# A transformer's attention layer: where weights are measured, and which score blocks go to VectorE

## The chip, the cores and the metric

The kernel runs on one core of a Trainium2 chip. The core has TensorE (matrix products, PE in the profile; its weight loads are PEld), VectorE (DVE), ScalarE (ACT), GpSimd (POOL) and SyncE (SP, which here only issues DMAs). GpSimd issues DMAs as well. Each engine takes its instructions in the order in which the program lists them, and waits on semaphores for the others. The metric is the device time of one execution in microseconds, median over runs.

## The reference

Two identical layers are applied to x of 2048 tokens by 448 features: attention with 16 heads of 28 features, then a gated linear unit of width 1792. All is float32.

```
x = x + A(layernorm(x), wqkv, wo)
x = x + B(layernorm(x), w_gate, w_up, w_down)
x = x + A(layernorm(x), wqkv, wo)
x = x + B(layernorm(x), w_gate, w_up, w_down)

A: q, k, v = split(x @ wqkv);  p = softmax(q k^T / sqrt(28));  (p v) @ wo
B: (sigmoid(x @ w_gate) * (x @ w_up)) @ w_down
```

## The kernel before

**Numbers in two halves.** Products are computed in float16 with each operand split into a high and a low half. To split a weight, it is first scaled by a power of two that comes from its sum of squares. So each weight is read once to be *measured* (its sum of squares is added up in a column of the tile `sums`: column 3 for wo, 4 for w_gate, 5 for w_up, 6 for w_down), and read again to be *split*; the split parts go to DRAM (`o_parts`, `dn_parts`, `gu_parts`) and are used in both layers.

**Stages.** Each layer is `project` (norm of x, products with wqkv), `attend`, `out_project` and `gated`. The two layers run one after the other. In `project` the tokens come in four blocks b1, b2, b3 after the first; `qk` makes seven tiles of q and k for a block, and after the evacuation of tile i it calls `fill[i]`, a piece of work for a later block: norms, `squares` (scaling and transposing a block into xs), `store` (xs to DRAM), `gather` (back into xraw in another order), `ready` (split). `vals` makes the values. Tile i of q and k is evacuated by ScalarE (L757, L760) and VectorE (L758, L762), and its squares are summed over heads on TensorE three tiles later (L736, L739); the last three of a block are summed in `finish`, which `qk` of the next block calls after its tile 1. TensorE writes its tiles into four PSUM banks in turn.

**Attention.** Time is counted in chunks c = 16 h + kc: head h, keys 128 kc to 128 kc + 127. A chunk has four units, one for each 512 queries. `score` computes three units' scores on TensorE and their exponentials in one instruction on ScalarE (L1179); `mix` multiplies a chunk's probabilities with the values on TensorE (L1215), some two groups behind. The string `FEW` (L68) says for each head of layer 0 how many of its 64 units are computed by VectorE instead (`score_aside`, ten instructions from L1189 to L1198, with a polynomial for the exponential); in layer 1 it is three in every head. `ASIDE` (L67) says where: with two units in a head, the first is begun at chunk 4 of the head and needed at chunk 10, the second begun at chunk 9 and needed at chunk 15. When a head's last chunk is mixed, `finish` (six instructions from L1244 to L1250 on VectorE) reads the head's sum from its PSUM bank, divides and stores.

The banks matter for what follows. Two banks serve the sums of even and odd heads in turn, and a head's units on VectorE use the bank of the other parity, so the first unit of head h + 1 takes the bank in which the sum of head h lay:

```
ps = bank(1 - u // (NT * NB) % 2, "aside")      # in score_aside
accs[h] = bank(h % 2, "acc")                    # in mix
```

**The weights' preparation.** `Prepare` is made at chunk 4 of layer 0. It holds a list of steps, each with the chunk at which it is put into the program, after that chunk's mix (and after `finish` where that chunk ends a head): first twelve measures (wo at chunk 6, w_down in four pieces at 10, 14, 18, 22, gate-and-up in seven tiles at 26 and every five chunks, to 56), at 61 `sizes` and the split of wo, from 66 seven splits of w_down, one every 8 chunks, from 122 fourteen splits of gate and up, one every 7; the end is at 220. A step issues the read of the next step's weights on GpSimd's queue first, and the write of the step before. Two buffers take the reads in turn. VectorE does all of the measuring (`add`, L1053 and L1055) and splitting. `sizes` (L1066) adds `sums` over the partitions with an instruction of GpSimd (L1067), and VectorE turns the results into powers of two (L246, L248).

**Slots.** Large tiles live in 19 equal slots; `Slots.get` takes the slot that has been free longest, and a tile in it waits for the last reader of the tile before.

What the program order around a chunk is can be read in these lines of `mix`, `along` and `Prepare.along`:

```
if kc == NT - 1:
    finish(h)
along(c)
...
while self.steps and self.steps[0][0] <= c:
    self.steps.popleft()[1]()
```

Of the kernel before, what the change touches and what calls it, by code (L numbers as in the profile page):

```python
# [64 lines left out]


ASIDE = {1: ((6, 15, 1),), 2: ((4, 10, 3), (9, 15, 1)), 3: ((4, 9, 3), (8, 13, 1), (12, 15, 2))}  # L67
FEW = "2221212111111233"  # L68


TAIL = (0, 1, 3, 2, 5, 4, 6)
# [47 lines left out]
def interleaved_layers(ctx: ExitStack, tc: tile.TileContext, x_in, wqkv, wo, w_gate, w_up,  # L119
# [88 lines left out]
    def load_rows(dst, src, c0, n, queue=nc.sync, parted=False):  # L208

        for a, b in ((0, 2), (2, 3)) if parted else ((0, 3),):  # L210
            queue.dma_start(dst[:, a:b, :],
                            src[a * P:b * P, c0:c0 + n].rearrange("(s p) n -> p s n", p=P))
        queue.dma_start(dst[0:64, 3, :], src[384:448, c0:c0 + n])
        queue.dma_start(dst[64:128, 3, :], src[384:448, c0:c0 + n])
# [48 lines left out]
    class Block:  # L263
# [337 lines left out]
    class WeightsQKV:  # L601
# [111 lines left out]
    def project(layer, wq, begun):  # L713
# [109 lines left out]
        if layer == 0:  # L823
            def scaled():
                b1.xn = big.get("xn", [P, TB, D])
                for j in range(TB):
                    b1.scale(j)

            def turned(kts):
                b1.turn_banks(6, kts)  # L830
                for j in range(TB):
                    b1.turn(j)
                b1.turned_high()
                b1.turned_low()

            fill = [idle, idle, lambda: b1.norm([0, 1]), lambda: b1.norm([2, 3]), idle, scaled]
            along_values = {0: lambda: (b1.parts(), turned([0, 1])),
                            1: lambda: (turned([2, 3]), big.put(b1.xn)),
                            2: lambda: (fin(), b2.norm()),
                            3: lambda: (b2.squares(), b2.store())}  # L840
        else:
            ones_of_values()
            fill = [idle, lambda: b1.ready(0, 1), lambda: b1.ready(2, 3), b2.norm,
                    lambda: b2.squares([0, 1]), sq(2, 2, 3), b2.store]
            along_values = {0: b3.norm, 1: lambda: (fin(), sq(3, 0, 1)()), 2: b2.gather,
                            3: sq(3, 2, 3)}
# [72 lines left out]

        return values, heads, last_values  # L920

    def true_maxima(h):
# [24 lines left out]
    class Prepare:  # L947


        def __init__(self):  # L950
            nc.vector.memset(sums[:, 3:7], 0.0)
            self.part = cpool.tile([P, 2], F32, name="part", tag="part", bufs=1)
            self.raws, self.packs = big.ring(2), big.ring(2)
            self.halves, self.half = None, 0
            tiles = [("o", 0)] + [("d", j) for j in range(4)] + [("gu", j) for j in range(7)]
            order = [(self.measure, what) for what in tiles] + [
                (self.split, what) for what in tiles[:1] + [("w", p) for p in range(NP)] + [
                    (w, p) for p in range(NP) for w in ("g", "u")]]
# [12 lines left out]
            self.pack = None  # L971
# [10 lines left out]
        def read(self, kind, j):  # L982
            if kind in "wgu" and len(kind) == 1:
                if self.halves is None:
                    self.halves = big.at(self.raws, "raws", [P, 2, 1024])
                self.half = 1 - self.half
                self.next = self.halves[:, self.half]
            else:
                self.next = big.at(self.raws, "raw", [P, 2048])
            if kind == "o":  # L990
                load_rows(self.view(self.next, kind), wo, 0, D, nc.gpsimd)
            elif kind == "gu":
                for i, w in enumerate((w_gate, w_up)):
                    load_rows(self.view(self.next, kind)[:, i], w, j * 2 * P, 2 * P, nc.gpsimd)
            elif kind == "w":
                for z in range(2):
                    r = slice((z * NP + j) * P, (z * NP + j + 1) * P)
                    nc.gpsimd.dma_start(self.view(self.next, kind)[:, z], w_down[r])
            elif kind in "gu":
# [7 lines left out]
            else:  # L1007
                n = self.count(j)
                nc.gpsimd.dma_start(self.view(self.next, kind)[:, 0:n, :],
                                    w_down[j * 512:j * 512 + n * P, :].rearrange(  # L1010
                                        "(s p) n -> p s n", p=P))

        def count(self, j):
            return min(4, NF - 4 * j)

        def view(self, t, kind):
            if kind == "gu":
# [32 lines left out]
        def add(self, m, v):  # L1050
            junk = big.at(self.packs, "junk", [P, 2048], BF16)
            n = v.free_size()
            nc.vector.tensor_tensor_reduce(junk[:, 0:n], v, v, 1.0, sums[:, m:m + 1],  # L1053
                                           op0=ALU.mult, op1=ALU.add, accum_out=self.part[:, 0:1])
            nc.vector.tensor_copy(sums[:, m:m + 1], self.part[:, 0:1])  # L1055

        def measure(self, raw, kind, j):
            if kind == "o":
                self.add(3, raw[:, 0:4 * D])
            elif kind == "gu":  # L1060
                self.add(4, raw[:, 0:1024])
                self.add(5, raw[:, 1024:2048])
            else:
                self.add(6, raw[:, 0:self.count(j) * D])

        def sizes(self):  # L1066
            nc.gpsimd.partition_all_reduce(size[:, 3:7], sums[:, 3:7], channels=P,  # L1067
# [770 lines left out]
```

## Time and profile before

| | us |
|---|---|
| median of 3 runs | 1909.33 (1908.06 to 1909.71) |
| the profiled execution | 1909.05 |
| its span | 1907.3 |
| first exponential of layer 0 starts | 120.23 |
| first weights read for `Prepare` issued | 117.27 |

Times in a profile are microseconds from the start of the span. A row of the stretches has the stretch, its length, then busy time and count of TensorE's matmuls, of its weight loads, of VectorE, ScalarE and GpSimd, the granted TensorE clock, the DMA engines' share and GB/s. A row of the groups has line, engine, operation, output and inputs, the count, then total busy time, the mean in ns, and the idle time before with what ended it. A row of a timeline has start, duration, engine, line, operation, shapes, and in brackets the idle time before it and what ended it; an engine ending in q is a queue. In the DMA rows the last number is the median time from issue to landing. TensorE's matmuls are pipelined and their ends modelled, so rows of it overlap, and a busy TensorE needn't be at its peak.

### The profile page before, as it was taken

The numbers are of one execution on the slowest core, as the hardware profiler recorded it, in microseconds if no ns is written. First come the engines' busy times: TensorE is split into PE (matmuls) and PEld (weight loads), VectorE is DVE, ScalarE is ACT, GpSimd is POOL, SyncE is SP. The second block draws the span as 40 slices with busy tenths as digits, with TensorE's granted clock in tenths as the row PEclk, the third lists the DMA queues.
The fourth block names the chain that finished last, engine by engine and source line by source line (L and its number), as shares of the span: only waits on it lengthen the run. The fifth ranks groups of instructions, "written<-read, shape, count | busy, mean of one in ns | idle before, by whom it ended". The sixth has DMA issues, their size and how long they took to land. (4 is left out here: it accounts for less than half of the span.)

```text
span 1907.3 us, 56306 instructions
## 1 busy us (share of the span) xinstructions
PE 1894.4 (99%) x24281; PEld 1402.4 (74%) x24281; DVE 1392.1 (73%) x2768; ACT 1386.7 (73%) x1772; POOL 255.3 (13%) x523
## 2 busy tenths in 40 slices
PE   9999999999999999999999999999999999999999
PEld 4455555555566789999954568888888767899998
DVE  7648798697886688787564487787778676887664
ACT  5569999999993556555344799999999645565541
POOL 2013312232102211213100000000000021121110
PEclk9999999999999999999999999999999999999999
DMA  5565554445213565656734321122121244666553
GB/s 174 165 206 159 154 164 140 128 139 158 90 64 111 181 212 220 220 198 218 264 107 127 95 51 43 35 51 51 29 49 48 79 132 141 223 245 223 213 206 141
DMA packets 107953, 269.79 MB, mean 141 GB/s; under 512 B 12894, under 2 KB 64222, under 8 KB 107568
## 3 DMA queue, kind: packets, MB, share of 16 engines
q0 software_dynamic: 32592, 162.18, 24.0%
q1 hardware_dynamic: 74768, 103.71, 19.2%
q8 instruction: 191, 3.13, 0.7%
q14 instruction: 66, 0.54, 0.1%
q10 hardware_dynamic: 336, 0.23, 0.0%
HBM read 207.88 MB, written 50.85 MB: 136 GB/s over the span
## 5 line engine op out<-in xcount | busy, mean ns | idle before, releaser
L1179 ACT ACTIVATE prob_s<-sc 128x1536 f32<-128x1536 f32 x659 | 892.2, 1486 | 6.8 <-DMA qp_s<-qk_scr 3.6
L1215 PE MATMUL acc<-prob_s,val_s 128*32 128x256 f32 (+3 forms) x7754 | 595.2, 383 | 0.0
L1164 PE MATMUL sc<-qp_s 114*32 114x512 f16 x7896 | 580.0, 379 | 0.0
L580 PEld LDWEIGHTS <-gu_s 128*128 128x128 f16 x4368 | 426.6, 98 | 54.7 <-issue 5.9
L1164 PEld LDWEIGHTS <-qp_s 114*32 114x32 f16 x8192 | 310.0, 95 | 177.2 <-issue 77.7
L1215 PEld LDWEIGHTS acc<-prob_s,val_s 128*32 128x32 f32 x7754 | 323.7, 110 | 95.7 <-issue 7.3
L580 PE MATMUL chain<-xwide_s,gu_s 128*128 128x256 f16 x2016 | 248.1, 273 | 3.1 <-ACT one_q L1566 2.0
L1493 PE MATMUL dnp<-dn_s,hparts_s 128*128 128x224 f16 x2016 | 225.2, 259 | 0.0
L1493 PEld LDWEIGHTS <-hparts_s 128*128 128x128 f16 x2016 | 194.0, 98 | 4.5
L1566 ACT COPY one_q<-chain 128x256 f32<-128x256 f32 x224 | 82.2, 372 | 122.3 <-PE chain L580 121.8
L1195 DVE SCALAR_TENSOR_TENSOR power_q<-power_q,expo_q 128x512 f32<-128x512 f32 x222 | 153.7, 692 | 7.6
L1582 DVE TENSOR_TENSOR one_q<-side,one_q 128x512 f32<-128x512 f32 x112 | 72.2, 686 | 98.6 <-PE side L580 98.5
L580 PE MATMUL side<-xshort_s,gu_s 128*128 128x256 f16 x1120 | 140.8, 273 | 1.5 <-DVE one_q L1582 1.5
L565 PE MATMUL qkp<-xhl_s,wqk_s 128*128 128x512 f16 x616 | 138.0, 379 | 0.7 <-DVE xhl_s L544 0.3
L565 PEld LDWEIGHTS <-wqk_s 128*128 128x128 f16 x616 | 60.0, 98 | 70.2 <-ACT wqk_s L231 1.1
L1380 POOL DMA_DIRECT2D gu_s<-gu_parts x104 | 56.0, 538 | 415.2 <-PE side L580 387.6
L1244 DVE STREAM_TRANSPOSE oturned_q<-acc 128x512 f32<-128x512 f32 x32 | 22.9, 716 | 117.8 <-PE acc L1215 117.8
L580 PE MATMUL side<-xwide_s,gu_s 128*128 128x256 f16 x672 | 91.7, 273 | 0.3
L757 ACT ACTIVATE qkhl_q<-qkp 128x512 f16<-128x512 f32 x56 | 33.2, 593 | 75.1 <-PE qkp L565 71.7
L1446 ACT CAST hparts_s<-hsums_q 128x256 f16<-128x256 f32 (+1 forms) x136 | 65.3, 494 | 29.9 <-DVE hsums_q L1458 20.6
L1215 PE MATMUL acc<-power_q,val_s 128*32 128x256 f32 (+3 forms) x278 | 86.4, 393 | 0.0
L1593 ACT ACTIVATE one_q<-one_q 128x512 f32<-128x512 f32 x56 | 35.2, 629 | 64.8 <-DVE one_q L1582 64.8
(213 smaller groups left out, 2327.6 us busy)
## 6 DMA issues: line engine op xcount, KB each, us to landing
gu_s<-gu_parts POOLq DMA_DIRECT2D x104, 800.0 KB, 5.8
dn_s<-dn_parts POOLq DMA_DIRECT2D x42, 784.0 KB, 7.6
qp_s<-qk_scr SPq DMA_DIRECT2D x96, 224.0 KB
qk_scr<-qkhl_q SPq DMA_DIRECT2D x56, 256.0 KB
gu_parts<-pack_s POOLq DMA_DIRECT2D x14, 800.0 KB, 3.8
xt_scr<-xs_s SPq DMA_DIRECT2D x48, 224.0 KB
xraw_s<-xt_scr SPq DMA_DIRECT2D x12, 768.0 KB
qp_s<-qk_scr SPq DMA_DIRECT2D x64, 112.0 KB
```

The source lines that it names most:

```text
L565: nc.tensor.matmul(pm, w, x, start=(i == 0), stop=(i == len(terms) - 1))
L580: nc.tensor.matmul(pm, a, x, start=(first and i == 0), stop=(i == len(terms) - 1), skip_group_check=True)
L1164: nc.tensor.matmul(ps[32 * j:32 * j + 32, :], hd.k[:, keys], hd.q[:, qb * W:(qb + 1) * W], start=True, stop=True, tile_position=(0, 32 * j))
L1179: nc.scalar.activation(prob[:, 0:n, :], ps[:, 0:n, :], AF.Exp, scale=exp_scale)
L1195: nc.vector.scalar_tensor_tensor(p, p, c[k], y, op0=ALU.add, op1=ALU.mult)
L1215: nc.tensor.matmul(acc[qb * VC:(qb + 1) * VC, s], v[:, kc % TB, h, :], probs[c * NB + qb][:, s], start=(kc == 0 and a == 0), stop=(kc == N ...
L1380: queue.dma_start(self.gu[-1][m], gu_parts[p, m])
L1446: nc.scalar.copy(to[:, :, 0], a)
L1493: nc.tensor.matmul(pm, a[:, x, t], w[:, p, y], start=(begin and n == 0 and (j == 0 or alone)), stop=(n == 2), skip_group_check=True)
L1566: nc.scalar.copy(to, pm)
L1582: nc.vector.tensor_tensor(one[m], side[m], one[m], op=ALU.add)
L1593: nc.scalar.activation(out, v, AF.Sigmoid, scale=gate_scale)
```

## The change

Half of the measuring moves from attention into the projection of layer 0. A new class `Measure` reads wo, the four pieces of w_down and the first gate-and-up tile during the first block's values (`along_values`, all on GpSimd's queue), and adds up their squares after tiles 4, 5 and 6 of block 2 and tiles 0, 1 and 2 of block 3; the second half of the gate-and-up tile is squared by ScalarE. It holds six slots for the weights and one for the instruction's unused output meanwhile.

`Prepare` keeps six gate-and-up tiles to measure, at chunks 6, 10, 14, 18, 22 and 26; `sizes` and the split of wo come at chunk 30 instead of 61; the splits of w_down start at 35 and come every 10 chunks instead of 8, those of gate and up start at 105 and come every 9 instead of 7; the end is at 231 instead of 220.

`FEW` gives two units to every head of layer 0 but the last, which has three: 33 instead of 26. Heads 3, 5 and 7 to 12 gain one, head 14 loses one.

```diff
-FEW = "2221212111111233"
+FEW = "2222222222222223"
...
-            along_values = {0: lambda: (b1.parts(), turned([0, 1])),
-                            1: lambda: (turned([2, 3]), big.put(b1.xn)),
-                            2: lambda: (fin(), b2.norm()),
-                            3: lambda: (b2.squares(), b2.store())}
+            tell = Measure()
+            along_values = {0: lambda: (b1.parts(), turned([0, 1]), tell.read(2)),
+                            1: lambda: (turned([2, 3]), big.put(b1.xn), tell.read(2)),
+                            2: lambda: (fin(), b2.norm(), tell.read()),
+                            3: lambda: (b2.squares(), b2.store(), tell.read())}
...
-        fin = qk(2, b2, [idle, lambda: b3.ready(0, 1), lambda: b3.ready(2, 3)], None)
-        fin = qk(3, blks[3], [], fin)
+        add = tell.add if layer == 0 else idle
+        fin = qk(2, b2, [idle, lambda: b3.ready(0, 1), lambda: b3.ready(2, 3), idle, add, add,
+                         add], None)
+        fin = qk(3, blks[3], [add, add, add], fin)
...
+    class Measure:
+        def __init__(self):
+            nc.vector.memset(sums[:, 3:7], 0.0)
+            self.part = cpool.tile([P, 2], F32, name="part0", tag="part", bufs=1)
+            self.junk = big.get("junk", [P, 2048], BF16)
+            self.to_read = deque([("o", 0)] + [("d", j) for j in range(4)] + [("gu", 0)])
+            self.rows = deque()
...
+        def add(self):
+            kind, t, n = self.rows.popleft()
+            m, n = {"o": (3, n), "d": (6, n), "gu": (4, 1024)}[kind]
+            v = t[:, 0:n]
+            nc.vector.tensor_tensor_reduce(self.junk[:, 0:n], v, v, 1.0, sums[:, m:m + 1],
+                                           op0=ALU.mult, op1=ALU.add,
+                                           accum_out=self.part[:, 0:1])
+            nc.vector.tensor_copy(sums[:, m:m + 1], self.part[:, 0:1])
+            if kind == "gu":
+                junk = qrt.get("junk", [P, 1024], BF16)
+                nc.scalar.activation(junk, t[:, 1024:2048], AF.Square, accum_out=sums[:, 5:6])
...
     class Prepare:
         def __init__(self):
-            nc.vector.memset(sums[:, 3:7], 0.0)
...
-            tiles = [("o", 0)] + [("d", j) for j in range(4)] + [("gu", j) for j in range(7)]
+            tiles = [("gu", j) for j in range(1, 7)]
...
-                at += ((5 if what[0] == "gu" else 4) if do == self.measure else
-                       {"o": 5, "w": 8}.get(what[0], 7))
+                at += 4 if do == self.measure else {"o": 5, "w": 10}.get(what[0], 9)
```

More of the change, by code (lines that the diff above doesn't have):

```diff
@@ L920, in project, with read @@
         return values, heads, last_values
+    class Measure:
[5 more added lines that the diff above has]
+            self.rows = deque()
+        def read(self, n=1):
+            for _ in range(n):
+                kind, j = self.to_read.popleft()
+                t = big.get("raw", [P, 2048])
+                n = {"o": 4, "d": min(4, NF - 4 * j), "gu": 0}[kind]
+                v = t[:, 0:n * D].rearrange("p (s n) -> p s n", n=D)
+                if kind == "gu":
+                    v = t.rearrange("p (w s c) -> p w s c", w=2, s=4)
+                    for i, w in enumerate((w_gate, w_up)):
+                        load_rows(v[:, i], w, 0, 2 * P, nc.gpsimd)
+                elif kind == "o":
+                    load_rows(v, wo, 0, D, nc.gpsimd)
+                else:
+                    nc.gpsimd.dma_start(v, w_down[j * 512:j * 512 + n * P, :].rearrange(
+                        "(s p) n -> p s n", p=P))
+                self.rows.append((kind, t, n * D))
+        def add(self):
[6 more added lines that the diff above has]
+            nc.vector.tensor_copy(sums[:, m:m + 1], self.part[:, 0:1])
+            if kind == "gu":
+                junk = qrt.get("junk", [P, 1024], BF16)
+                nc.scalar.activation(junk, t[:, 1024:2048], AF.Square, accum_out=sums[:, 5:6])
+                qrt.put(junk)
+                big.put(self.junk)
+            big.put(t)
     def true_maxima(h):
@@ L954, in __init__ @@
             self.halves, self.half = None, 0
-            tiles = [("o", 0)] + [("d", j) for j in range(4)] + [("gu", j) for j in range(7)]
+            tiles = [("gu", j) for j in range(1, 7)]
             order = [(self.measure, what) for what in tiles] + [
-                (self.split, what) for what in tiles[:1] + [("w", p) for p in range(NP)] + [
+                (self.split, what) for what in [("o", 0)] + [("w", p) for p in range(NP)] + [
                     (w, p) for p in range(NP) for w in ("g", "u")]]
@@ L998, in read @@
                     nc.gpsimd.dma_start(self.view(self.next, kind)[:, z], w_down[r])
-            elif kind in "gu":
+            else:
                 v, w = self.view(self.next, kind), {"g": w_gate, "u": w_up}[kind]
@@ L1006, in read @@
                 nc.gpsimd.memset(v[64:P, 3], 0.0)
[L1007 to L1014, printed above, removed]
         def view(self, t, kind):
@@ L1057, in measure @@
         def measure(self, raw, kind, j):
[L1058 to L1064, printed above, removed]
+            self.add(4, raw[:, 0:1024])
+            self.add(5, raw[:, 1024:2048])
         def sizes(self):
```

## The prediction

> **What bounds the kernel now.** I read the page's first part, then the busy time in stretches of 20 us, then the groups of attention in each layer, then the timelines of VectorE, TensorE and GpSimd where the change acts.
>
> ```profile
> span 1907.3 us, 56306 instructions
> PE 1894.4 (99%) x24281; PEld 1402.4 (74%) x24281; DVE 1392.1 (73%) x2768; ACT 1386.7 (73%) x1772; POOL 255.3 (13%) x523
> ...
> 40.00:60.00 20.00, 20.00 (x100) 9.59 (x98) 17.36 (x42) 8.45 (x14) 2.42 (x4) 1.00 0.34 78
> ...
> 80.00:100.00 20.00, 20.00 (x99) 9.51 (x98) 10.86 (x24) 11.79 (x21) 0.00 (x0) 1.00 0.35 119
> ...
> 200.00:220.00 20.00, 20.00 (x364) 11.54 (x360) 16.37 (x30) 20.00 (x16) 7.23 (x12) 1.00 0.64 174
> ...
> 380.00:400.00 20.00, 20.00 (x376) 11.16 (x371) 19.53 (x45) 20.00 (x16) 5.22 (x9) 1.00 0.45 140
> ...
> L1179 ACT ACTIVATE prob_s<-sc 128x1536 f32<-128x1536 f32 x332 | 447.5, 1518 | 3.8 <-DMA qp_s<-qk_scr 3.3 <-PE sc L1164 0.3
> ...
> L1179 ACT ACTIVATE prob_s<-sc 128x1536 f32<-128x1536 f32 x325 | 443.3, 1457 | 2.9 <-PE sc L1164 2.6 <-DMA qp_s<-qk_scr 0.3
> ```
>
> In the projection (the first two stretches) TensorE is busy 20.00 of 20 us; VectorE has 2.6 us of room in the one and 9.1 in the other. In layer 0's attention ScalarE is busy 20.00 of 20 us: 447.5 / 332 = 1.348 us for each group of three units. In layer 1, with three units a head on VectorE, a group takes 443.3 / 325 = 1.364 us: ScalarE does less there and something else (TensorE, as full as its rows can show) sets 61 / 3 x 1.364 = 27.7 us a head. VectorE is not a bound by share, but at 19.53 of 20 us it has no room in some heads, and its queue is in order. The profiled execution took 1909.05 us, 1.75 more than its span and 0.28 under the median 1909.33; the sum is made against 1909.05.
>
> **What the change gains.** VectorE takes 33 units of layer 0 instead of 26. ScalarE loses 7 / 3 groups: 2.33 x 1.348 = -3.15 us. A head with two units then lasts 62 / 3 x 1.348 = 27.86 us on ScalarE, just above the 27.7, so the gain is not cut by TensorE.
>
> **What it adds to the projection.** VectorE gets five sums of squares and half of a sixth, under tiles 4 to 6 of block 2 and 0 to 2 of block 3.
>
> ```profile
> 44.20 0.20 POOL L291 TENSOR_SCALAR rs<-mv 128x4 f32<-128x4 f32 x1 [14.30 <-DVE mv L288]
> 54.56 0.19 POOL L291 TENSOR_SCALAR rs<-mv 128x4 f32<-128x4 f32 x1 [9.06 <-DVE mv L288]
> 56.42 0.65 DVE L338 STREAM_TRANSPOSE xs_s<-xn_s 128x448 f32<-128x448 f32 x1
> 57.08 0.38 SPq L358 DMA_DIRECT2D xraw_s<-xt_scr  x1
> 64.92 0.28 DVE L762 TENSOR_TENSOR sq_q<-sq_q 128x256 bf16<-128x256 bf16 x1
> 66.06 0.49 PE L739 MATMUL knorm<-sq_q,ind 128*128 128x256 bf16 x3
> 83.44 0.28 DVE L762 TENSOR_TENSOR sq_q<-sq_q 128x256 bf16<-128x256 bf16 x1
> 90.38 0.49 PE L739 MATMUL knorm<-sq_q,ind 128*128 128x256 bf16 x3
> 103.73 0.69 DVE L758 SCALAR_TENSOR_TENSOR qkhl_q<-qkp,qkhl_q 128x512 f16<-128x512 f32 x1 [1.53 <-ACT qkhl_q L757]
> ...
> 142.98 2.08 DVE L1053 CUSTOM_DVE_ANT_0 junk_s<-raw_s,sums 128x1792 bf16<-128x1792 f32 x1
> 145.10 0.15 DVE L1055 COPY sums<-part 128x1 f32<-128x1 f32 x1
> 145.29 2.08 DVE L1053 CUSTOM_DVE_ANT_0 junk_s<-raw_s,sums 128x1792 bf16<-128x1792 f32 x1
> 171.59 1.14 DVE L1053 CUSTOM_DVE_ANT_0 junk_s<-raw_s,sums 128x896 bf16<-128x896 f32 x1
> 202.29 1.28 DVE L1053 CUSTOM_DVE_ANT_0 junk_s<-raw_s,sums 128x1024 bf16<-128x1024 f32 x1
> 205.38 1.29 DVE L1053 CUSTOM_DVE_ANT_0 junk_s<-raw_s,sums 128x1024 bf16<-128x1024 f32 x1
> ```
>
> A sum over 1792 columns takes 145.29 - 142.98 = 2.31 us, one over 896 about 1.37, half a gate-and-up tile 3.09 / 2 = 1.54: together 4 x 2.31 + 1.37 + 1.54 = 12.2 us. A tile's own two operations take 0.69 + 0.28. From 83.72 (end of tile 4's), two sums and two tiles end at 83.72 + 4.62 + 1.94 = 90.28; TensorE wants tile 6's squares at 90.38. By tile 6 of block 3 it is 83.72 + 12.2 + 8 x 0.97 + 0.8 (two maxima) = 104.5, against 103.73. TensorE has four banks in turn, so this costs 0 to 0.8 us; I take 0. ScalarE's one square of 1024 columns (under the 1.348 us of an exponential of 1536) lies in its 8.2 idle us of 20. GpSimd issues 4 reads in its idle 14.30 us before 44.20 and 7 in the 9.06 before 54.56, at 0.8 us each or less (L211 below): no norm waits behind them.
>
> Seven more slots are held here (six weight tiles, one for junk). Counting the free slots through the program, block 3's transposes get the slot that block 2's have just left, so VectorE waits at 56.42 for that store to land (the gather, which waits for the same, goes at 57.08): 0.66 us. TensorE needs the squares of 64.92 + 0.28 at 66.06, slack 0.86, so nothing is lost unless the store itself is late. The reads of w_down's end and of the first gate-and-up tile go out on GpSimd's queue just ahead of it and can hold it by up to 2 us: cost 0 to 2 + 0.66 - 0.86 = 1.8. The DMA engines are busy 0.34 of this stretch, so I take 0.3, nearer the lower end.
> [...] No run here shows these reads beside the store.
>
> **What it does to heads 0 to 2.** Here lies the price. Six gate-and-up measures now run at chunks 6, 10 ... 26, then at chunk 30 `sizes` (GpSimd's reduction over partitions, for which VectorE waits) and the split of wo; before, these two came at chunk 61, in a head with one unit.
>
> ```profile
> 136.69 0.75 DVE L1189 TENSOR_SCALAR expo_q<-aside,base 128x512 f32<-128x512 f32 x1 [3.02 <-PE aside L1164]
> 151.07 2.08 DVE L1053 CUSTOM_DVE_ANT_0 junk_s<-raw_s,sums 128x1792 bf16<-128x1792 f32 x1 [3.50 <-DMA raw_s<-in_B_w_down_dram]
> 153.27 0.71 DVE L1244 STREAM_TRANSPOSE oturned_q<-acc 128x512 f32<-128x512 f32 x1
> 155.26 0.40 PE L1164 MATMUL aside<-qp_s 114*32 114x512 f16 x4
> 156.84 0.75 DVE L1189 TENSOR_SCALAR expo_q<-aside,base 128x512 f32<-128x512 f32 x1
> 180.28 0.72 DVE L1244 STREAM_TRANSPOSE oturned_q<-acc 128x512 f32<-128x512 f32 x1 [4.25 <-PE acc L1215]
> 181.54 0.83 PE L1164 MATMUL sc<-qp_s 114*32 114x512 f16 x12
> 182.19 0.40 PE L1164 MATMUL aside<-qp_s 114*32 114x512 f16 x4
> ...
> 233.03 0.17 DVE L246 TENSOR_SCALAR pw<-size 128x4 int32<-128x4 int32 x1 [5.82 <-POOL size L1067]
> 236.69 0.71 DVE L1244 STREAM_TRANSPOSE oturned_q<-acc 128x512 f32<-128x512 f32 x1
> ...
> 232.55 0.44 POOL L1067 PARTITION_ALL_REDUCE size<-sums x1 [6.52 <-issue]
> ...
> 165.51 0.77 POOL L211 DMA_DIRECT2D raw_s<-in_B_w_gate_dram  x1 [11.34 <-DVE sums L1055]
> 168.63 0.52 POOL L214 DMA_DIRECT2D raw_s<-in_B_w_up_dram  x1
> ...
> raw_s<-in_B_w_gate_dram POOLq DMA_DIRECT2D x14, 64.0 KB, 4.4
> ```
>
> Prices: a unit on VectorE 142.98 - 136.69 = 6.29; a head's `finish` 156.84 - 153.27 = 3.57; a gate-and-up measure 205.38 - 202.29 = 3.09; the wait for the reduction 5.82; sizes and the split of wo 236.69 - 233.03 = 3.66. A read of a weight tile starts when the measure two before it is done, and lands after 151.07 - 145.25 = 5.8 us (one transfer) or 168.63 - 165.51 + 4.4 = 7.5 (six transfers): my bounds.
>
> VectorE's queue after the change, with 5.8 (in brackets 7.5): unit of head 0 done at 142.98; two measures to 149.16; the third waits for its read, issued at 146.0 (the first two go out before attention starts, as two reads did): 151.8 to 154.9 (156.6); `finish` of head 0 to 158.5 (160.2); unit 164.8; measure 167.9; unit 174.2; two measures 180.4 (182.1); reduction 186.2 (187.9); sizes and wo 189.9 (191.6). Only then `finish` of head 1 reads its bank, which TensorE had ready at 180.28. TensorE needs that bank for head 2's first unit (score_aside takes the bank that head 1's sum lies in), at 182.19, and everything behind it on TensorE waits, scores for ScalarE among it. The bank is free at 189.9 + 0.72 = 190.6 (192.3): TensorE goes on 8.4 (10.1) us late. ScalarE is covered for about 1.35 - 0.83 = 0.5 us, by the scores already written. Loss 7.9 to 9.6; I take the middle, 8.7: the third read has the size of the first row's and the transfers of the second's. VectorE then runs ahead again, since head 2 comes as late as its work.
> [...]
>
> **What it does to heads 3 to 14.** A split now comes every 10 chunks (w_down) or 9 (gate, up) instead of 8 and 7.
>
> ```profile
> 328.96 0.74 DVE L1189 TENSOR_SCALAR expo_q<-aside,base 128x512 f32<-128x512 f32 x1
> 335.81 0.42 DVE L1047 TENSOR_TENSOR sums_q<-raws_s 128x256 f32<-128x256 f32 x1
> 341.08 0.47 DVE L234 SCALAR_TENSOR_TENSOR pack_s<-raws_s,up,pack_s 64x256 f16<-64x256 f32 x1
> ```
>
> A split takes 341.55 - 335.81 = 5.74 us. A head holds 2 x 6.29 + 3.57 + 16/9 x 5.74 = 26.4 us of VectorE in 27.86; with units at 335.81 - 328.96 = 6.85, 27.5. It fits, barely; I take 0. The last split ends before chunk 231 instead of 220, 25 chunks (44 us) before the end of attention.
>
> **The sum.** 1909.05 - 3.15 + 8.7 + 0.3 = 1914.9: 1915.
>
> **Rivals.** (1) *No stall: the gain comes through.* VectorE reaches head 1's `finish` in time, or TensorE does not need the bank. Against it: with no wait for the third read `finish` of head 0 starts at 153.27 as before, and the same sum runs 156.84, 163.2, 166.2, 172.6, 178.7, 184.6, 188.2: the bank is still 6.7 us late. For it: in the trace before, VectorE sat idle 4.25 us before 180.28 in this very head, so small errors of the queue have some room. Time 1909.05 - 3.15 + 0.3 = 1906.2. It decides once L1244 starts before 182.19 + 0.5 - 0.72 = 182.0. (2) *Half a stall.* The 5.82 us are mostly GpSimd's own delay before chunk 61 and shrink to its 0.44; then the read of wo (issued at 177.3, landed at 183.1) and 3.66 end at 186.8, the bank is free at 187.5, loss 5.3 - 0.5 = 4.8: 1911.0. For it: GpSimd was issuing reads shortly before; against: VectorE's wait was the whole 5.82. (3) *VectorE overloads in heads 6 to 14.* A split just ahead of `finish` holds the bank by up to 5.74 + 0.72 - 1.9 (180.28 to 182.19) = 4.5 us; half of that in half of nine heads adds 10: 1925. For it: 98.6% at 6.85 a unit; against: 19.53 of 20 us ran without a gap on ScalarE. (4) *The projection pays in full*, 0.8 + 1.8: 1917.2.
>
> **Chances.** Forecast 0.56; rival 1 0.13, 2 0.11, 3 0.12, 4 0.08. Against no change a measurement here can tell about 0.2%, 3.8 us: slower means over 1913.1, faster under 1905.5. Slower: forecast, 3 and 4, less 0.04 for a queue that errs by a microsecond or two at the forecast's lower end (1909.05 - 3.15 + 7.9 = 1913.8): 0.72. Within: rival 2, 0.08 of rival 1 and that 0.04: 0.23. Faster: what is left of rival 1, 0.05. The forecast's own range is 1913.8 to 1917.3 (9.6 and 1.8); to 8 in 10 it takes in rivals 2 and 4 and half of 3: 1910 to 1920.
>
> **What would show it.** Right: a gap of 8 to 10 us in ScalarE's exponentials near 185 to 193 us, waited out on TensorE's scores, with L1244 of head 1 directly behind the split of wo; L246 with a wait near 5.8; two groups fewer in layer 0 (330 whole ones); elsewhere 1.35 a group. Wrong: L1244 of head 1 within 2 us of its sum, gaps in heads 6 to 14, or layer 0's exponentials starting later than 122 us.

## The result, and the profile after

| | before | after |
|---|---|---|
| median, us (7 runs each, same chip) | 1908.30 (1906.36 to 1909.71) | 1914.13 (1913.50 to 1915.82) |
| ratio | | 1.0029 (95%: 1.0018 to 1.0039) |
| profiled execution, us | 1909.05 | 1913.5 |
| its span, us | 1907.3 | 1911.8 |
| first exponential of layer 0 starts, us | 120.23 | 120.99 |

The kernel became slower by 5.8 us, and the forecast was 1915.0. Lines have moved: L1164, L1179, L1215, L1189, L1244, L1053 and L1067 of before are L1196, L1211, L1247, L1221, L1276, L1090 and L1099 now.

The page's first part, and the groups of ScalarE in layer 0's attention (120 to 578 us):

```profile
span 1911.8 us, 56315 instructions
PE 1890.9 (99%) x24249; PEld 1331.5 (70%) x24249; DVE 1431.8 (75%) x2835; ACT 1384.0 (72%) x1772; POOL 255.9 (13%) x523
...
L1211 ACT ACTIVATE prob_s<-sc 128x1536 f32<-128x1536 f32 x330 | 444.5, 1513 | 13.8 <-PE sc L1196 13.6
L1211 ACT ACTIVATE prob_s<-sc 128x512 f32<-128x512 f32 x1 | 0.6, 628 | 0.0
```

The last group of before, beside the 332 whole ones (447.5 us) that the prediction shows:

```profile
L1179 ACT ACTIVATE prob_s<-sc 128x1024 f32<-128x1024 f32 x1 | 1.0, 1049 | 0.0
```

ScalarE has less to do: 444.5 + 0.6 = 445.1 us instead of 447.5 + 1.0. The seven units are therefore worth 3.4 us. But ScalarE is idle for 13.8 us instead of 3.8 in the same stage, nearly all of it waiting for TensorE's scores. Nearly all of these 10.0 us lie in one place. The timeline of VectorE there:

```profile
152.86 1.28 DVE L1090 CUSTOM_DVE_ANT_0 junk_s<-raw_s,sums 128x1024 bf16<-128x1024 f32 x1 [2.71 <-DMA raw_s<-in_B_w_gate_dram]
...
155.92 0.71 DVE L1276 STREAM_TRANSPOSE oturned_q<-acc 128x512 f32<-128x512 f32 x1
...
181.04 0.15 DVE L1092 COPY sums<-part 128x1 f32<-128x1 f32 x1
187.25 0.17 DVE L246 TENSOR_SCALAR pw<-size 128x4 int32<-128x4 int32 x1 [6.06 <-POOL size L1099]
...
187.74 1.14 DVE L229 TENSOR_SCALAR pack_s<-raw_s,up 128x1792 f16<-128x1792 f32 x1
188.92 2.08 DVE L234 SCALAR_TENSOR_TENSOR pack_s<-raw_s,up,pack_s 128x1792 f16<-128x1792 f32 x1
190.92 0.71 DVE L1276 STREAM_TRANSPOSE oturned_q<-acc 128x512 f32<-128x512 f32 x1
```

VectorE's last measure ends at 181.19; then it waits 6.06 us for GpSimd's reduction, splits wo, and only at 190.92 reads the bank of head 1's sum. TensorE, in the same stretch:

```profile
182.89 0.83 PE L1196 MATMUL sc<-qp_s 114*32 114x512 f16 x12
191.68 0.62 PE L1196 MATMUL aside<-qp_s 114*32 114x512 f16 x4 [7.96 <-DVE oturned_q L1276]
...
192.91 1.52 PE L1196 MATMUL sc<-qp_s 114*32 114x512 f16 x12
```

Head 2's first unit waits 7.96 us for that bank, and with it everything behind it on TensorE. One thing was not foreseen: the twelve matmuls of a group's scores, 0.83 us at 182.89, take 1.52 at 192.91. The stretches of two microseconds show why (the last columns are granted clock, DMA share, GB/s):

```profile
182.00:184.00 2.00, 1.72 (x28) 0.79 (x21) 0.00 (x0) 2.00 (x3) 0.00 (x0) 1.00 0.42 116
184.00:186.00 2.00, 0.00 (x0) 0.00 (x0) 0.00 (x0) 1.42 (x2) 0.00 (x0) 0.98 0.00 0
186.00:188.00 2.00, 0.00 (x0) 0.00 (x0) 0.71 (x6) 0.00 (x0) 1.21 (x3) 0.50 0.00 0
...
194.00:196.00 2.00, 2.00 (x29) 1.10 (x24) 1.93 (x4) 1.45 (x1) 0.00 (x0) 0.50 0.92 287
196.00:198.00 2.00, 2.00 (x44) 1.06 (x40) 1.90 (x4) 1.25 (x1) 0.00 (x0) 0.96 0.46 143
```

TensorE's granted clock falls from 1.00 to 0.50 while it idles and stays there after it has gone on, until about 196. On ScalarE this shows as a second, smaller gap:

```profile
194.54 1.45 ACT L1211 ACTIVATE prob_s<-sc 128x1536 f32<-128x1536 f32 x1 [9.12 <-PE sc L1196]
196.75 5.65 ACT L1211 ACTIVATE prob_s<-sc 128x1536 f32<-128x1536 f32 x4 [0.76 <-PE sc L1196]
```

Outside layer 0's attention, two differences can be placed. The first exponential comes 0.76 us later. The first 30 us of the kernel differ from execution to execution, so the projection is better counted from a row just ahead of the first new read: GpSimd's `rs<-mv` of two columns (L291), at 28.91 us before and at 28.81 after. From there to the first exponential it is 91.3 us before and 92.2 after, 0.9 longer. In the ten profiles with this projection unaltered it is 91.9 to 92.4, in the two with the old one 91.1 and 91.3, while the row itself lies anywhere from 28.66 to 31.51. And in the stages from 640 us on, where nothing was changed, TensorE's waits are fewer. The view of TensorE's waits there, before and then after (line, what was waited for, us in total, times, longest):

```profile
PE side L580 <- DVE one_q L1582: 1.5, 4, 0.8
PE chain L580 <- DMA gu_s<-gu_parts: 1.1, 2, 0.9
PE chain L580 <- ACT one_q L1566: 1.0, 1, 1.0
```

```profile
PE chain L580 <- ACT one_q L1598: 1.0, 1, 1.0
PE side L580 <- DVE one_q L1614: 0.5, 2, 0.3
```

That is 2.1 us less. Summed: 10.0 - 3.4 + 0.76 - 2.1 = +5.3, where the spans differ by 4.5; 0.8 us are not placed. (The medians differ by 5.8: of the two profiled executions the one of before lies 0.75 us above its median, the other 0.6 below.)

### The profile page after: what moved, and what is told of

Read it like the earlier page. It is cut to its first block, busy times and chain, and to the rows that moved or that the text cites. A ratio compares the mean times of both kernels' runs of the same rounds, so it can differ in the third digit from the quotient of the medians.

```text
span 1911.8 us, 56315 instructions
## 1 busy us (share of the span) xinstructions
PE 1890.9 (99%) x24249; PEld 1331.5 (70%) x24249; DVE 1431.8 (75%) x2835; ACT 1384.0 (72%) x1772; POOL 255.9 (13%) x523
## 3 DMA queue, kind: packets, MB, share of 16 engines
q8 instruction: 192, 3.15, 0.7%
## 5 line engine op out<-in xcount | busy, mean ns | idle before, releaser
L1211 ACT ACTIVATE prob_s<-sc 128x1536 f32<-128x1536 f32 (+1 forms) x657 | 888.1, 1483 | 17.3 <-PE sc L1196 13.9
L1247 PE MATMUL acc<-prob_s,val_s 128*32 128x256 f32 (+3 forms) x7700 | 573.4, 384 | 0.0
L1196 PE MATMUL sc<-qp_s 114*32 114x512 f16 x7868 | 556.0, 379 | 0.0
L1196 PEld LDWEIGHTS <-qp_s 114*32 114x32 f16 x8192 | 277.1, 96 | 208.9 <-issue 93.3
L1247 PEld LDWEIGHTS acc<-prob_s,val_s 128*32 128x32 f32 x7700 | 276.8, 110 | 141.3 <-issue 14.1
L1227 DVE SCALAR_TENSOR_TENSOR power_q<-power_q,expo_q 128x512 f32<-128x512 f32 x243 | 168.2, 692 | 8.3
L1276 DVE STREAM_TRANSPOSE oturned_q<-acc 128x512 f32<-128x512 f32 x32 | 22.9, 717 | 95.8 <-PE acc L1247 95.6
L1247 PE MATMUL acc<-power_q,val_s 128*32 128x256 f32 (+3 forms) x300 | 94.2, 396 | 0.0
```

Of the source, the lines that this page charges most:

```text
L1196: nc.tensor.matmul(ps[32 * j:32 * j + 32, :], hd.k[:, keys], hd.q[:, qb * W:(qb + 1) * W], start=True, stop=True, tile_position=(0, 32 * j))
L1211: nc.scalar.activation(prob[:, 0:n, :], ps[:, 0:n, :], AF.Exp, scale=exp_scale)
L1227: nc.vector.scalar_tensor_tensor(p, p, c[k], y, op0=ALU.add, op1=ALU.mult)
L1247: nc.tensor.matmul(acc[qb * VC:(qb + 1) * VC, s], v[:, kc % TB, h, :], probs[c * NB + qb][:, s], start=(kc == 0 and a == 0), stop=(kc == N ...
```

## The experiments

The theory: the price is VectorE's queue at the end of head 1 (a wait for GpSimd and a split ahead of `finish`), and the half clock behind it. The rivals: VectorE's load as such, so that the wait would come back elsewhere; a clock that falls for another reason; reads that cost the projection more than the queue does. Each kernel is the changed one with the edit shown, unless it says otherwise. The kernel before ran beside each: 1909.4 us beside the first eight runs, 1909.1 beside the next three, 1908.3 beside the last.

**The reduction early, the rest behind `finish`.**

```diff
                 if i == len(tiles) - 1:
                     self.steps.append((at, self.sizes))
+                    at += 4
+                    self.steps.append((at, self.powers_of_sizes))
...
                                            reduce_op=ReduceOp.add)
+
+        def powers_of_sizes(self):
             powers(3, 4, size[:, 3:7])
```

The `at += 4` also makes every later split come four chunks later: the last comes at chunk 226 instead of 222.

> GpSimd's reduction over the partitions stays at chunk 30; what VectorE does with its result (the powers, the factors) and the split of wo move to chunk 34, behind head 1's finish (chunk 31). Theory, the queue: head 1's finish and head 2's first unit aside no longer stand behind a VectorE that waits 6 us for GpSimd and then splits wo. TensorE's wait ahead of that unit (7.96 us in the changed kernel) falls below 1 us, its clock stays at 1.00 between 184 and 198 us, and the 10.3 us that head 2 took beyond the others go: 1914.1 - 10.3 = 1903.8 us, between 1903 and 1905.5. Rival, the load: two units per head and the preparation fill VectorE in heads 0 to 2, so the same wait comes back one or two chunks later, and the time stays above 1910.

1903.33 us (1902.70 to 1903.92), 0.9967 of before (0.9955 to 0.998): 10.8 us below the changed kernel. VectorE's timeline:

```profile
181.16 0.15 DVE L1094 COPY sums<-part 128x1 f32<-128x1 f32 x1
181.74 0.72 DVE L1280 STREAM_TRANSPOSE oturned_q<-acc 128x512 f32<-128x512 f32 x1 [0.42 <-PE acc L1251]
...
191.60 0.16 DVE L246 TENSOR_SCALAR pw<-size 128x4 int32<-128x4 int32 x1
```

Now VectorE waits 0.42 us for head 1's sum, not TensorE for VectorE, and when it comes to the powers at 191.60 the reduction is long done: a step with no wait. Every stretch from 182 to 198 has TensorE busy throughout, at clock 1.00. The work in these heads is the same, only its order differs, so the rival of the load as such falls.

**Only the split of wo behind `finish`.**

```diff
                 if i == len(tiles) - 1:
                     self.steps.append((at, self.sizes))
+                    at += 2
```

> Reduction and VectorE's part of it stay together at chunk 30, ahead of head 1's finish; only the split of wo goes behind that finish (chunk 32). Theory, the queue: the wait is shorter by the split's two rows (1.14 + 2.08 = 3.2 us): 7.96 - 3.2 = 4.7 us. TensorE still idles longer than the 2.3 us after which its clock was seen at half, so the loss to the clock stays about as it was (1.9 to 2.3 us), and the time is 1914.1 - 3.2 = 1910.9. If the clock's loss shrinks with the idle time: 1909.5 to 1910.5. Rival, the load: 1913 to 1914, since the split only goes to a place that is as full.

1911.31 us (1909.52 to 1912.20). On TensorE:

```profile
188.69 0.62 PE L1197 MATMUL aside<-qp_s 114*32 114x512 f16 x4 [4.89 <-DVE oturned_q L1277]
...
189.93 1.52 PE L1197 MATMUL sc<-qp_s 114*32 114x512 f16 x12
```

The wait is 4.89 us where 4.7 were expected, and the clock falls all the same (0.50 in every microsecond from 188 to 194; 1.52 us for twelve matmuls). So the split was worth its two rows, 3.07 us for 3.22, the wait for the reduction makes up most of the rest, and this shorter idle time does not spare the clock.

**TensorE kept busy in the gap: 32 matmuls, then 112.**

```diff
         def score_aside(u):
+            if layer == 0 and u == (2 * NT + 10) * NB + 3:
+                spare = triple((now + 1) % 2, "spare")
+                for _ in range(8):
+                    scores(spare[:, 0, :], u)
...
         for g in range(2, groups + 3):
+            now = g
             more(g)
```

> Changed kernel, with 32 more matmuls (the 4 of head 2's first unit aside, 8 times over, into a free bank of three that nothing reads) right ahead of that unit, where TensorE idles for 7.96 us. At 0.83 us for 4 they take 6.6 us of the idle time. Theory: TensorE lost its clock because it idled, and 1.9 to 2.3 us of the stall are the slow matmuls behind the wait. Kept busy, its clock stays at 1.00 up to 198 us, the wait shrinks to about 1 us, the unit still starts at about 191.7 us, and the time is 1912.0 (1911.7 to 1912.4). Rival: the clock falls for another reason, or the exponentials behind the wait were slow for another engine's sake: 1914, or up to 1 us more if the 32 matmuls hold up something.

1919.62 us (1918.13 to 1920.65). Missed: the filler was sized at 0.83 us for four matmuls, but the rows of scores with 0.83 us have twelve of them (a row of four has 0.40, or 0.62 at half clock). At 0.83 for twelve, 32 take 2.2 us; they took 1.91, not 6.6:

```profile
185.61 1.91 PE L1196 MATMUL spare<-qp_s 114*32 114x512 f16 x32 [0.41 <-ACT prob_s L1211]
193.46 0.62 PE L1196 MATMUL aside<-qp_s 114*32 114x512 f16 x4 [5.93 <-DVE oturned_q L1280]
```

TensorE still idled for 5.93 us, and the clock fell (0.50 in every microsecond from 193 to 199). Of the 5.5 us above the changed kernel only 1.8 are idle time of ScalarE in this stage (15.6 us instead of 13.8): in the stages from 640 us on, TensorE's waits for VectorE's `one_q` and for `gu_s` stand at 1.5 and 1.3 us in this profile, near those of the kernel before (1.5 and 1.1), where the changed kernel has 0.5 and none. Another 0.8 us stand ahead of the first exponential (121.79). Together that is 4.9 of the 5.3 us by which the two spans differ. With `range(28)`, and the unaltered changed kernel on the same chip:

> As the run with 32 matmuls in the idle time, but with 112: those 32 took 1.91 us, 0.06 each since four of them run side by side, and left TensorE idle for 5.93 us behind them. 112 take 6.7 us. Theory: the clock stays at 1.00 up to 200 us (it was at half for 10.2 us in the changed kernel, and for 6.8 us with 32), the unit still starts at about 192, and the time is 2 us below the unaltered changed kernel (1.5 to 2.4). Rival: the slow matmuls behind the wait are no part of what the stall costs, since the exponentials would have waited for VectorE's bank anyway: the time is the same within 0.5 us, with the clock at 1.00.

> The changed kernel once more, unaltered, as the mark on this chip for the three kernels that run beside it: 1913 to 1916 us, with the clock at half for about 10 us behind 186 us.

1914.12 us (1913.26 to 1914.76) unaltered, 1912.48 (1911.33 to 1913.51) with 112. The timeline of TensorE and the stretches of that run:

```profile
184.79 6.23 PE L1196 MATMUL spare<-qp_s 114*32 114x512 f16 x112 [0.39 <-ACT prob_s L1211]
192.38 0.40 PE L1196 MATMUL aside<-qp_s 114*32 114x512 f16 x4 [1.37 <-DVE oturned_q L1280]
...
193.03 0.83 PE L1196 MATMUL sc<-qp_s 114*32 114x512 f16 x12
```

```profile
186.00:190.00 4.00, 4.00 (x84) 2.20 (x76) 1.98 (x7) 0.08 (x1) 2.22 (x3) 1.00 0.18 47
190.00:194.00 4.00, 2.63 (x52) 1.42 (x48) 3.90 (x5) 0.02 (x1) 1.61 (x3) 1.00 0.48 168
```

The clock stays at 1.00, the unit waits for the same bank, the twelve matmuls behind it take 0.83 us again, and the time falls by 1.6 us. That is the price of the half clock: work that does nothing made the kernel faster.

**The old list of units, with the stall and without.**

```diff
-FEW = "2222222222222223"
+FEW = "2221212111111233"
```

> Changed kernel with the old list of units aside (2221212111111233), 7 units fewer; heads 0 to 2, with the stall, are as in the changed kernel. Theory, the prediction's sum: 7/3 groups of 1.348 us come back, 1914.1 + 3.15 = 1917.3. By the head times of the two profiles, in which heads 3 to 15 took 4.2 us less: 1918.3. Rival: VectorE's load with two units per head costs the changed kernel something in heads 3 to 14, and the old list gives it back: below 1916.

1921.79 us (1919.39 to 1922.53), 7.7 above the changed kernel: missed, by twice what either count gave. The profiled spans differ by 7.4: 3.6 us of exponentials (447.6 + 1.1 for 445.1), 0.7 of ScalarE's idle time in the stage (14.5 for 13.8), 2.0 of TensorE's waits from 640 us on (1.5 for `one_q` and 1.0 for `gu_s`, instead of 0.5 and none) and 0.1 ahead of the first exponential; 1.0 is not placed. Behind the stall ScalarE has no gap:

```profile
198.99 382.02 ACT L1211 ACTIVATE prob_s<-sc 128x1536 f32<-128x1536 f32 x284 [0.22 <-PE sc L1196]
```

The same edit on the kernel with the reduction early:

> The run with the reduction early (1903.3 us, without the stall) with the old list 2221212111111233: what seven units more are worth where nothing stalls. Theory, the sum with TensorE's floor: a head with one unit takes 28.25 us and one with two 27.77 (0.48 for a unit), head 14 with three 27.62, no less than TensorE needs: 8 x 0.48 - 0.15 = 3.7, so 1907.0 (1906.6 to 1907.4). By the prediction's term (7/3 groups of 1.348 us): 1906.5. Rival: the run with the stall and the old list lay 7.7 us above the changed kernel; if that is what the units are worth, 1911.

1912.74 us (1910.60 to 1915.34), 9.4 above that kernel. The second run's profile, ScalarE's groups and its timeline near the end of the stage:

```profile
L1215 ACT ACTIVATE prob_s<-sc 128x1536 f32<-128x1536 f32 x332 | 447.4, 1518 | 6.9 <-PE sc L1200 6.5 <-DMA qp_s<-qk_scr 0.3
L1215 ACT ACTIVATE prob_s<-sc 128x1024 f32<-128x1024 f32 x1 | 1.0, 1044 | 0.0
```

```profile
540.02 9.55 ACT L1215 ACTIVATE prob_s<-sc 128x1536 f32<-128x1536 f32 x7 [0.63 <-PE sc L1200]
551.49 24.10 ACT L1215 ACTIVATE prob_s<-sc 128x1536 f32<-128x1536 f32 x18 [1.92 <-PE sc L1200]
```

With the reduction early and the new list:

```profile
L1215 ACT ACTIVATE prob_s<-sc 128x1536 f32<-128x1536 f32 x330 | 444.0, 1521 | 4.1 <-PE sc L1200 4.0
L1215 ACT ACTIVATE prob_s<-sc 128x512 f32<-128x512 f32 x1 | 0.6, 632 | 0.0
```

So the units are worth 448.4 - 444.6 = 3.8 us; the prediction's term had 3.15. Another 2.8 are idle time, most of it (0.63 and 1.92) at the end of head 14, which has three units in the old list. The last split lies in that head, since with this edit the splits come four chunks later: it ends at 537.37, two units follow on VectorE without a gap until 550.05, and TensorE waits 1.3 us for the second one. In the run with the stall, where the last split comes at chunk 222, in head 13, that gap is missing. With the new list and the later splits it is missing too (the kernel with the reduction early). So in these profiles it belongs to the old list and the later splits together, not to either alone. The waits of the stages from 640 us on add 1.9: they stand at 1.3 and 1.1 again, where the new list has 0.5 and none. These are differences of two profiled executions, and that of the old list (1915.34 us) is its slowest, 11.9 above the other (1903.46). 2.5 of the 11.9 stand ahead of the first exponential (123.45 and 120.99), nearly all of it ahead of the first new read (L291 at 31.51 and 28.90), where the two kernels are alike. That places 11.0 of 11.9; of the 9.4 between the medians, the three terms above are 8.5.

**The new list without the spread** (the kernel before, with only that line changed):

> The kernel before, with the new list of units aside (2222222222222223) and nothing else: all sums of squares stay in head 0 to 3, with the splits every 7 or 8 chunks. Theory (VectorE's load decides how many units a head may have): from head 6 on the splits leave too little of VectorE for two units each, a unit's result or the bank of a unit comes late at some three or four places in heads 7 to 15, 2 to 4 us each, and the time is above that of before by 4 to 8 us: 1913 to 1917. Rival: the splits were not dense enough for that, and the seven units more are a plain gain: 1909.4 - 3.2 to 3.8 = 1905.6 to 1906.2; then the new spread of the splits was needless.

1916.10 us (1914.96 to 1916.76). VectorE and TensorE where head 9 ends:

```profile
409.90 0.47 DVE L234 SCALAR_TENSOR_TENSOR pack_s<-raws_s,up,pack_s 64x256 f16<-64x256 f32 x1
410.41 0.72 DVE L1244 STREAM_TRANSPOSE oturned_q<-acc 128x512 f32<-128x512 f32 x1
```

```profile
411.18 0.62 PE L1164 MATMUL aside<-qp_s 114*32 114x512 f16 x4 [4.87 <-DVE oturned_q L1244]
```

Two splits run without a gap from 398.54 to 410.37, `finish` stands directly behind them, and the bank is 4.87 us late; the same happens once more near 500 us (8.9 us in both), and ScalarE idles 17.1 us in the stage instead of 3.8. This is the third rival of the prediction. The kernel before, with one unit in these heads and the splits at the same chunks, has no such gap, so here VectorE's load decides. The changed kernel, with the new list and the spread, has none either. That the spread avoids it by its lower rate, and not by where its splits fall in the heads, is not shown.

**The sixth read later, and earlier.**

```diff
-                            3: lambda: (b2.squares(), b2.store(), tell.read())}
+                            3: lambda: (b2.squares(), b2.store())}
...
-            ... lambda: (b2.ready(2, 3), b3.store())]
+            ... lambda: (b2.ready(2, 3), b3.store(), tell.read())]
```

> Changed kernel, with the read of the sixth tile (the first tile of w_gate and w_up) moved from behind block 2's store to behind block 3's store, so that block 3's transposed copy no longer gets the slot that the store of block 2's is just leaving. Theory: the 0.89 us for which VectorE waited there (57.57 us) goes, and with it most of the 0.76 us by which the first exponential came later: first exponential at about 120.3 us instead of 121.0, time 0.5 to 0.8 us below the unaltered changed kernel. Rival: the 0.76 us come from the six sums on VectorE (12.2 us more) or from the DMA traffic of the reads beside the projections; then the first exponential stays at 121.0, and the time the same within 0.3 us.

1914.67 us (1913.85 to 1916.79) against 1914.12: no gain. VectorE and ScalarE in the changed kernel, then ScalarE in this one:

```profile
57.57 0.65 DVE L338 STREAM_TRANSPOSE xs_s<-xn_s 128x448 f32<-128x448 f32 x1 [0.89 <-DMA xt_scr<-xs_s]
...
62.83 1.14 ACT L218 CAST xhl_s<-xraw_s 128x512 f16<-128x512 f32 x2 [4.10 <-DMA xraw_s<-xt_scr]
```

```profile
64.44 1.14 ACT L218 CAST xhl_s<-xraw_s 128x512 f16<-128x512 f32 x2 [5.42 <-DMA xraw_s<-xt_scr]
```

The wait of 0.89 us for the slot is gone, as expected, and with it two waits of TensorE (0.20 and 0.30 us, shown below). But ScalarE now waits 1.3 us longer for block 2's gather, beside which the read comes to lie, VectorE waits for ScalarE, and TensorE for VectorE's squares:

```profile
68.03 0.27 PE L739 MATMUL knorm<-sq_q,ind 128*128 128x256 bf16 x1 [1.14 <-DVE sq_q L762]
```

In this profile the new place costs more than the old one gives back.

**Two steps more on the best version:** the measures at chunks 6, 10, 16, 19, 23, 27, and then the sixth read one tile earlier as well.

```diff
-                at += 4 if do == self.measure else {"o": 5, "w": 10}.get(what[0], 9)
+                at += (4, 6, 3, 4, 4, 3)[i] if do == self.measure else (
+                    {"o": 5, "w": 10}.get(what[0], 9))
```

> As the run with the reduction early and the rest behind head 1's finish (1903.3 us), and the measures moved too: chunks 6, 10, 16, 19, 23, 27 instead of 6, 10, 14, 18, 22, 26, so that the third, which waits for its read (2.71 us on VectorE), comes behind head 0's finish (chunk 15) and not ahead of it; VectorE's part and wo at chunk 33. Theory, the queue: the bank of head 1's first unit comes in time, and head 1, which took 28.66 us where the others with two units take 27.76, gives back up to 0.9: 1902.4 to 1902.9. Rival: the wait for the read is then met by another piece of the queue, and the time is 1903.3 within 0.3.

> As the run before it in this list, with the sixth read issued one value tile earlier (two reads behind block 2's norm, none behind its store). Theory by the run that moved this read the other way (it met block 2's gather, ScalarE's wait for it went from 4.10 to 5.42 us, and the first exponential came 0.4 us later than in the unaltered kernel beside it): what the projections lose is DMA traffic beside block 2's store and gather, so a read that is through before them gives back 0.3 to 0.7 us, the first exponential at 120.5 to 120.9. Rival: the six reads cost the same wherever they lie: first exponential at 121.0 to 121.4, time the same within 0.3.

1903.92 us (1902.21 to 1904.89), 0.9973 of before (0.9962 to 0.9984), and 1904.15 (1902.41 to 1905.29). In the first of the two, `finish` of head 0 starts at 152.47, ahead of the third measure, and ScalarE idles 3.4 us in the stage instead of 4.1; the profiled span is 1.2 us shorter, but the medians don't show it. The read makes no difference: the first exponentials come at 120.61 and 120.63, 91.9 and 91.8 us after GpSimd's row. The 120.63 alone would have fitted the theory, but the run without the earlier read has the same; what the rival said of the read holds, its 121.0 to 121.4 does not.

**Two units in the last head too**, on the kernel with the reduction early.

> The run with the reduction early (1903.3 us), with two units in the last head as well instead of three. What is asked is where the waits of the gated stages come from (TensorE for gu_s, 1.1 us, and for one_q, 1.5 us, in the kernel before and in both runs with the old list; 0 and 0.5 in eight of the nine runs with the new one). Theory: the size of layer 0's last exponential decides (two units are left over in the old list, one in the new one, two here), by when the stages behind it start: the waits come back, and the time is 1903.3 + 0.5 (one unit more on ScalarE) + 2.1 = 1905.9. Rival: something else of the old list or of the program's length decides: no such waits, 1903.8.

1903.94 us (1903.02 to 1904.68), with waits of 0.5 us for `one_q` and none for `gu_s`: the rival. What makes the stages from 640 us on up to 2 us longer in the three kernels with the old list, and in the one with 32 spare matmuls but not in the one with 112, stays open; each of these kernels was profiled once.

## Why the prediction was right

**What bounds it, and the place of the loss: right, and shown.** One gap in ScalarE's exponentials near 185 to 194 us, waited out on TensorE, with head 1's `finish` directly behind the split of wo, 330 whole groups: all as the prediction listed. Taking the reduction's wait and the split away from that place took away 10.8 us. The wait was 6.06 us for 5.82, so rival 2 (GpSimd's delay shrinks to 0.44) falls, and with L1276 at 190.92 rival 1 too.

**The size of the stall: 10.0 us for 8.7.** The queue was forecast to give the bank free at 190.6 to 192.3 and TensorE to be 8.4 to 10.1 us late. It went on at 191.68 after 7.96 us: the third read came near the lower bound (its measure starts at 152.86, forecast 151.8, in an attention that starts 0.76 later). What the term lacked is the clock: 1.6 us, by the run with 112 matmuls. A chain of durations from the trace before had no row at half clock in it: the granted clock is 1.00 in all its stretches, and TensorE waits nowhere in these heads.

**The gain: 3.4 us for 3.15,** 3.8 without the stall. Right.

**The projection: 0.8 us for 0.3.** The slot wait is where it was forecast, 0.89 us for 0.66. That the reads could hold the store by up to 2 us more was the author's guess, which no row gave; the wait came out 0.23 us longer. What was mis-sized is the step behind it, that a slack of 0.86 us hides it: the prediction had looked at one set of squares, wanted at 66.06, and VectorE is late for two rows ahead of it. TensorE's waits in the changed kernel that the kernel before has not:

```profile
34.24 1.28 PE L509 MATMUL turn<-ident,xn_s 128*128 128x128 f32 x6 [0.25 <-DVE xn_s L321]
60.11 0.27 PE L736 MATMUL qnorm<-sq_q,ind 128*128 128x256 bf16 x1 [0.20 <-DVE sq_q L762]
62.87 0.35 PE L590 MATMUL vp<-wv_s,xhl_s 128*128 128x448 f16 x1 [0.30 <-DVE qkhl_q L758]
```

The last two are gone where the slot wait is gone, in the run with the read moved to the later place. The first was not counted at all: four scalings on VectorE took 2.04 us instead of 1.78 there, while GpSimd issued the first six DMAs of the reads (29.74 to 33.97 us; the prediction had counted four). VectorE's sums are absorbed as forecast: from its row of L736 at 78.93 us to that at 103.87 TensorE takes 24.94 us, as before (77.96 to 102.90). Rival 4, 2.6 us in all, was too much.

**Heads 3 to 14 at nothing: right.** The changed kernel's idle time on ScalarE is the 3.1 us ahead of the first group, the 9.12 and 0.76 of the stall, and 0.8 elsewhere. Rival 3 has its mechanism in this kernel, but only with the old spread.

**What was not in the sum at all** is the 2.1 us by which TensorE's waits in the later stages were shorter, for a cause that is open. By luck it offset the clock and the projection, so the forecast's time is nearer (1915.0 for 1914.13) than its terms deserve.

## What to carry to other kernels

Before moving a step forward in an in-order queue, ask which bank or buffer the next instruction behind it frees, and who wants it: the wait for a reduction that had cost nothing at chunk 61 cost 10 us at chunk 30, one chunk ahead of `finish`. The order was the same before: there too `finish` (236.69) came directly behind the split of wo, and TensorE did not wait. But VectorE's last measure had ended at 227.2, some 9 us before the head's sum; in the changed kernel it ended only as head 1's sum came in, near 181. Split such a step into the part that starts the slow engine and the part that uses its result, and put the waiter's own work between them. And when a stall of several microseconds on TensorE is priced, add what its clock loses: here 1.6 us behind a wait of 7.96.

## What the runs showed of the hardware

**TensorE's clock was at half for 10.2 us in the changed kernel, for 6.8 in two others.** Stretches of one microsecond bound the half-clock time: in the changed kernel

```profile
185.00:186.00 1.00, 0.00 (x0) 0.00 (x0) 0.00 (x0) 0.42 (x1) 0.00 (x0) 0.95 0.00 0
...
196.00:197.00 1.00, 1.00 (x20) 0.47 (x16) 0.93 (x3) 0.25 (x1) 0.00 (x0) 0.93 0.52 188
```

With 1.00 on one side and 0.50 on the other, a mean of 0.95 puts the fall at 185.90, and 0.93 the rise at 196.14: 10.2 us at half. TensorE was idle from 183.72 to 191.68, so the fall came 2.2 us into the idle time and the rise 4.5 us behind its end. In the run with 32 matmuls:

```profile
192.00:193.00 1.00, 0.00 (x0) 0.00 (x0) 1.00 (x2) 0.00 (x0) 0.00 (x0) 0.78 0.41 154
...
199.00:200.00 1.00, 1.00 (x20) 0.54 (x16) 0.97 (x2) 1.00 (x1) 0.00 (x0) 0.81 0.33 73
```

That is 192.56 to 199.38, 6.8 us: the fall 5.0 us into an idle time of 5.93, the rise 5.9 behind its end. With only the split of wo moved it is 6.8 as well (0.64 in the microsecond from 187 and 0.95 in that from 194 give 187.28 to 194.10): the fall 3.5 us into an idle time of 4.89, the rise 5.4 behind its end. In the run with 112 matmuls TensorE idled for 0.39 and 1.37 us there, and the clock was 1.00 from 182 to 202. What sets the moments of the fall and of the rise is not shown.

**Four scalings on VectorE took 2.04 us beside GpSimd's DMA issues, 1.78 without them.** The 2.04 us lie beside the end of six issues in the changed kernel; the kernel before has none there. Beside the next seven issues (45.64 to 50.16 us) only one of four scalings was longer, 0.55 us for 0.47. What made them longer is not shown: no run here has the issues without the traffic of their reads.

**A few spare matmuls, and stages far behind them.** Two kernels that differ by 80 matmuls near 185 us differ by 7.1 us in their medians, and by 6.1 in their profiled spans. ScalarE's idle time in layer 0's attention accounts for 3.4 (15.6 us with 32 matmuls, 12.2 with 112), about half of it the clock by the 1.6 us above; the waits for `one_q` and `gu_s` after 640 us for 2.3 (2.8 and 0.5); the time to the first exponential, where the kernels are alike, for 0.4 (121.79 and 121.38). Why those waits differ is open.
